# Attention plus MLP on one core: the per-unit maxima as one block-diagonal product of three float32r passes, placed between scores and products with v

## The chip, the cores and the metric

The kernel runs on one core of one Trainium2 chip. The metric is device time in microseconds (us), as the median of several runs; lower is better. Before the change it is 872.64 us (three runs, 872.33 to 872.99).

## The reference, cut to what matters

```python
xn = _layernorm(x)                        # x: 1 x 2048 x 448
q = (xn @ wq) -> 16 heads of Dh = 28;  k = xn @ wk;  v = xn @ wv     # one k and v for all heads
p = softmax(q k^T * Dh**-0.5);  o = p v                              # 2048 queries x 2048 keys per head
out = x + o @ wo + relu(xn @ w1) @ w2                                # w1: 448 x 1792
```

All of it is float32. A softmax does not change when one number is taken from all scores of a query. The kernel takes away a maximum over the first 32 keys only, so that the exponentials stay in range; any number near the true maximum would do. A flag at the end has the whole program run a second time with a maximum over all keys, if the sums have gone out of range. That second program (`HM == 64`) is built, but is not executed in the runs here.

## The kernel before, in words

**Stages.** First come the layer norm, the projections to q, k and v (each float32 number is split into a high and a low float32r part, `hi` and `lo`), and the MLP. They fill the span up to about 340 us. The attention follows, from 340 us to the end.

**Attention.** It is cut into 16 units, one for each of 4 query blocks (512 queries) and 4 groups of 4 heads. A unit has two halves of 8 key blocks (128 keys). In a half, TensorE (PE) makes 32 score tiles of 128 keys by 512 queries (L627), then the products with v (L496). The order of the scores is written out by hand in `HALVES`: `a` is a score tile that ScalarE (ACT) turns into exponentials straight from PSUM (L653, 19 in a half); `d` is a score tile that VectorE (DVE) copies from PSUM (L658, 13 in a half), and whose exponentials ACT makes later in SBUF (L673). `F` is one tile of the output projection of an earlier unit (L542, added up by DVE on L544). `R` starts the reciprocals (L517) and the normalization of the unit before.

**PSUM.** The `a` tiles have four buffers. The `d` tiles, the output projections, the maxima and the accumulator of the products with v share a ring of four banks, `d0` to `d3`: `d_tile()` takes the next name from the ring and puts it at the ring's end; the accumulator takes one with `keep=True`, and it comes back to the ring only when DVE has copied the accumulator out (`oS`, L499). So in all halves but the first unit's first, three banks go round, and a matmul into a ring tile waits until the tile three uses before it has been read.

**Operands.** `kst` holds the keys on 114 partitions: 28 rows of `hi`, 28 of `hi`, 28 of `lo`, 28 of `lo`, and two rows of ones. `qst[u]` holds a unit's queries against it: 28 rows each of `hi`, `lo`, `hi`, `lo` for four heads, loaded by four DMAs (`load_stack`, L377), and two rows for minus the maximum. A score is one float32r product over 114 rows.

**Maxima.** `maxima(u + 1)` runs in the first half of unit u, in the run of products with v, behind the first of them (`n == 1`, which is the last key block of unit u - 1). It takes one ring tile and makes, for each of the four heads, the scores of the first 32 keys in float32 (L387: 112 rows, 32 columns, 512 queries; a head has its own 32 columns of the array and 32 partitions of the tile). A float32 product is two matmul instructions in the profile. DVE then transposes (L404), reduces (L405), splits into two parts and transposes back (L406 to L408), and eight small DMAs put the result into the two rows of `qst[u + 1]` (L412). `maxima(0)` runs in the MLP.

**What sets the order.** Each engine works through its instructions in the program's order. All DMAs are issued by SyncE (SP), in that order. The pool of the attention's small tiles (`opool`, L476) lies where the MLP's tiles were; its first write, the memset of `wo` on GpSimd (POOL, L481), waits for the last matmul of the MLP.

Of the kernel before, what the change touches and what calls it, by code (L numbers as in the profile page):

```python
# [8 lines left out]
F32 = mybir.dt.float32  # L9
F32R = mybir.dt.float32r  # L10
# [36 lines left out]
def program(ctx: ExitStack, tc: tile.TileContext, HM, fine, x, wq, wk, wv, wo, w1, w2, out):  # L47
    nc = tc.nc
    P = 128
    S, D = x.shape  # L50
    DH = wk.shape[1]
# [3 lines left out]
    QB = 512  # L55
    NQB = S // QB
    TPB = QB // P
    HG = 4
# [12 lines left out]
    KQ = 4 * DH  # L71
    NU = NQB * NHG
    NA, ND, NST = 4, 4, 3
# [9 lines left out]
    def d_tile(keep=False):  # L83

        name = ring.pop(0)
        if not keep:
            ring.append(name)
        t = psD.tile([P, QB], F32, name=name)
        return (t, name) if keep else t
# [26 lines left out]
    qscr = dram.tile([NHG, 2, P, S], F32, name="qscr")  # L116
# [25 lines left out]
    MQ = HG * DH  # L142
# [53 lines left out]
    kstF = kst.bitcast(F32)  # L196
# [170 lines left out]
    units = [(b, g) for b in range(NQB) for g in range(NHG)]  # L367

    def load_stack(u):
        if u >= NU:  # L370
            return
        b, g = units[u]
        st = stacks.tile([P, HG, QB], F32R, name="qst")
        qst[u] = st
        for r in range(4):
            src = qscr[g, r % 2, 0:MQ, b * QB : (b + 1) * QB].rearrange("(j d) q -> d j q", d=DH)
            nc.sync.dma_start(st.bitcast(F32)[r * DH : (r + 1) * DH], src)  # L377

    def maxima(u):

        st = qst[u]

        def scores(kb):
            pm = d_tile()
            for j in range(HG):
                c = slice(32 * j, 32 * j + 32)
                nc.tensor.matmul(  # L387
                    pm[c], kstF[0:KQ, kb * 32 : kb * 32 + 32], st.bitcast(F32)[0:KQ, j], start=True, stop=True
                )
            return pm  # L390

        n = QB // 32
        nm = small.tile([P, n], F32, name="nm")
        nm2 = small.tile([P, 2, n], F32R, name="nm2")
        rows = small.tile([P, 2 * n], F32, name="rows")
        sc = scores(0)
        if HM > 1:
            top = small.tile([P, QB], F32R, name="tmp").bitcast(F32)
            nc.vector.tensor_copy(top, sc)
            for kb in range(1, HM):  # L400
                nc.vector.tensor_tensor(top, top, scores(kb), op=ALU.max)
            sc = top
        mt = small.tile([P, QB], F32R, name="tmp").bitcast(F32)
        nc.vector.transpose(mt, sc)  # L404
        nc.vector.tensor_reduce(nm, mt.rearrange("p (c k) -> p c k", k=32), axis=AX.X, op=ALU.max, negate=True)  # L405
        nc.vector.tensor_copy(nm2[:, 0], nm)  # L406
        nc.vector.tensor_tensor(nm2[:, 1], nm, nm2[:, 0].bitcast(F32), op=ALU.subtract)
        nc.vector.transpose(rows, nm2.rearrange("p s n -> p (s n)").bitcast(F32))  # L408
        for j in range(HG):
            for s in range(2):  # L410
                r = KQ + s
                nc.sync.dma_start(  # L412
                    st.bitcast(F32)[r : r + 1, j].rearrange("o (c q) -> o c q", q=32),
                    rows[32 * j + s * n : 32 * j + s * n + n],
                )
# [59 lines left out]
    ppool = ctx.enter_context(tc.tile_pool(name="ppool", bufs=P_BUFS, reuse_waits="tile"))  # L475
    opool = ctx.enter_context(tc.tile_pool(name="opool", bufs=2))  # L476

    g3 = opool.tile([P, NHG, D], F32, name="wo", bufs=1)
    woH = opool.tile([P, NHG, D], F32R, name="woH", bufs=1)
    woL = opool.tile([P, NHG, D], F32R, name="woL", bufs=1)  # L480
# [8 lines left out]
    def pv(u, kb, p):  # L489
        start, stop = kb == 0, kb == NKB - 1  # L490
        done = stop or u == NU - 1 and kb == KH - 2
        if start:
            o_acc[u] = d_tile(keep=True)
        o = o_acc[u][0]
        for j in range(HG):
            nc.tensor.matmul(o[32 * j : 32 * j + 32], vtile[:, kb, :], p[:, j], start=start, stop=done)  # L496
        if stop:
            oS = opool.tile([P, QB], F32, name="oS")
            nc.vector.tensor_copy(oS, o)  # L499
            ring.append(o_acc.pop(u)[1])  # L500
            o_sb[u] = oS
            dens(u)
# [32 lines left out]
    def o_proj(u, i):  # L535

        b, g = units[u]
        oH, oL = o_hl[u]
        py = d_tile()[:, 0:D]
        c = slice(i * P, (i + 1) * P)  # L540
        for n, (om, wm) in enumerate(((oH, woH), (oH, woL), (oL, woH))):
            nc.tensor.matmul(py, om[:, c], wm[:, g, :], start=n == 0, stop=n == 2)  # L542
        t = b * TPB + i
        nc.vector.tensor_tensor(acc[:, t, :], py, acc[:, t, :], op=ALU.add)  # L544
        if g == NHG - 1:
            nc.sync.dma_start(out[t * P : (t + 1) * P, :], acc[:, t, :])
# [21 lines left out]
    def last_run(u, run):  # L568

        for h, c in enumerate(halves):  # L570
            o = psA.tile([P, QB], F32, name="a")
            for n, (v, kb, p) in enumerate(run):
                for j in range(HG):
                    nc.tensor.matmul(  # L574
                        o[32 * j : 32 * j + 32, c], vtile[:, kb, :], p[:, j, c],
                        start=n == 0, stop=n == len(run) - 1,
                    )
            nc.vector.tensor_tensor(fin["o"][:, c], o[:, c], fin["o"][:, c], op=ALU.add)
            quotients(h, fin["o"][:, c])
# [39 lines left out]

    HALVES = "adadaadadaadadaFaaddadaaFadaaddaad", "adadadaadaaddaadaFadaadadaFaadaRdad"
    HA, KH = 19, NKB // 2
    todo, behind, ended = [], [], []

    def score(u, kb, j, p, pt):
        nc.tensor.matmul(  # L627
            pt, kst[0 : KQ + 2, kb * P : (kb + 1) * P], qst[u][0 : KQ + 2, j, :], start=True, stop=True
        )
        return p[:, j]  # L630

    def ends():

        for u in ended:
            recips(u)
            normalized(u)
            todo.extend((u, i) for i in range(TPB))
        ended.clear()

    for u in range(NU):  # L640
        last = u == NU - 1
        for half, order in enumerate(HALVES):
            ps, n_a, n_d = {}, 0, HA
            for k in order:
                if k in "ad":
                    n = n_a if k == "a" else n_d
                    kb, j = n // HG, n % HG
                    if kb not in ps:
                        ps[kb] = ppool.tile([P, HG, QB], F32, name="p")
                if k == "a":  # L650
                    pt = psA.tile([P, QB], F32, name="a")
                    p = score(u, half * KH + kb, j, ps[kb], pt)
                    nc.scalar.activation(p, pt, AF.Exp, scale=SCALE)  # L653
                    n_a += 1
                elif k == "d":
                    pt = d_tile()
                    p = score(u, half * KH + kb, j, ps[kb], pt)
                    nc.vector.tensor_copy(p, pt)  # L658
                    n_d += 1
                elif k == "R":  # L660
                    ends()
                else:
                    for _ in range(3 if last and half else 1):
                        if todo:
                            o_proj(*todo.pop(0))
            if last:
                ends()
            if half == 0 and u:
                load_stack(u + NST - 1)
            for c in halves if last and half else [slice(0, QB)]:  # L670
                for kb in range(HA // HG, KH):
                    p = ps[kb][:, max(HA - kb * HG, 0) : HG, c]
                    nc.scalar.activation(p, p, AF.Exp, scale=SCALE)  # L673
            run = behind + [(u, half * KH + kb, ps[kb]) for kb in range(KH)]
            behind = [] if half and u >= NU - 2 else [run.pop()]
            if last and half:
                last_run(u, run)
                break
            for n, (v, kb, p) in enumerate(run):
                if half == 0 and n == 1 and not last:  # L680
                    maxima(u + 1)
                pv(v, kb, p)
                if kb == NKB - 1:
                    ended.append(v)
            if last:
                put_by(u)
# [27 lines left out]
```

## Time and profile before

| | |
|---|---|
| median of three runs | 872.64 us (872.33 to 872.99) |
| the profiled execution | 873.85 us |
| its span, first to last instruction | 872.0 us |
| mean granted TensorE clock | 0.999 |
| maxima, L387 | 128 matmul instructions, 593 ns mean each (several overlap) |
| scores, L627 | 1024 matmul instructions (608 into `a`, 416 into `d`) |
| products with v, L496 | 1976 matmul instructions |

A row of a timeline holds the start in us from the span's beginning, the time from the first start to the last end, the engine, the line, the operation with out<-in, and a count if equal instructions follow each other; in brackets stands how long the engine was idle before it, and what ended that. PE are the matmuls, PEld the loads of their stationary operand, SPq the issues of DMAs. The duration of a matmul reaches over the start of the next ones, so that the pace is read from starts.

### The profile page before, as it was taken

Reading aid. Unit: us, or ns where it says so; the run is one execution under the profiler, and the core shown is the slowest. Engines: PE = TensorE matmul, PEld = TensorE weight load, DVE = VectorE, ACT = ScalarE, POOL = GpSimd, SP = SyncE. Lnnn points to the kernel's source line nnn. Section 1 sums busy time; section 2 is a strip of 40 time slices with the busy share of each in tenths; the row PEclk is TensorE's granted clock in tenths of the full one; section 3 lists DMA queues with packets and bytes.
Section 4 is the critical chain, followed back from the end, with each engine's and each line's share of the span. In section 5 each row is a group of like instructions: output and inputs, shape, how many; then the busy total and the mean of one; then the engine's idle time right before and its main releaser. Section 6 shows DMA issues by size and latency. Waiting matters only on the chain.

```text
span 872.0 us, 13147 instructions
## 1 busy us (share of the span) xinstructions
PE 864.4 (99%) x5062; PEld 580.1 (67%) x5062; DVE 488.9 (56%) x893; ACT 554.9 (64%) x856; POOL 112.2 (13%) x93
## 2 busy tenths in 40 slices
PE   9999999999999999999999999999999999999997
PEld 8788888888888887455455455465465465465464
DVE  6843343343333346566576576576576476476475
ACT  4541111111111114999999999999999999999894
POOL 2034212020202001201001001001001001101110
PEclk9999999999999999999999999999999999999999
DMA  7858050110000001102112023112023112021001
GB/s 216 282 205 167 17 133 1 46 28 18 1 1 1 0 2 38 44 2 55 34 26 56 14 66 76 34 25 56 14 65 77 30 29 55 15 66 34 14 14 46
DMA packets 37499, 45.87 MB, mean 53 GB/s; under 512 B 13640, under 2 KB 24072, under 8 KB 37264
## 3 DMA queue, kind: packets, MB, share of 16 engines
q1 hardware_dynamic: 37432, 44.98, 20.1%
q8 instruction: 41, 0.67, 0.3%
q14 instruction: 26, 0.21, 0.1%
HBM read 32.37 MB, written 12.18 MB: 51 GB/s over the span
## 4 chain that ended last, share of the span: by engine, by line
PE 97%; DVE 1%; ACT 1%; DMA 1%; issue 0%; SPq 0%
PE d L496 25%; PE a L627 17%; PE a L204 16%; PE a L440 12%; PE d L627 11%; PE d L542 4%; PE d L440 4%; PE a L209 4%; PE d L387 2%; PE a L288 1%; DMA acc<-in_A_x 1%; PE d L258 1%; PE a L574 1%; DVE qs L272 0%; ACT p L673 0%; ACT p L653 0%
## 5 line engine op out<-in xcount | busy, mean ns | idle before, releaser
L658 DVE COPY p<-d 128x512 f32<-128x512 f32 x416 | 258.6, 681 | 164.2 <-PE d L627 162.4
L653 ACT ACTIVATE p<-a 128x512 f32<-128x512 f32 x608 | 301.5, 696 | 41.5 <-PE a L627 41.5
L496 PE MATMUL d<-p,vtile 128*32 128x512 f32 x1976 | 221.6, 594 | 0.0
L627 PE MATMUL a<-qst,kst 114*128 114x512 f32 x608 | 217.5, 403 | 0.0
L673 ACT ACTIVATE p<-p 128x2048 f32<-128x2048 f32 (+2 forms) x132 | 198.9, 1733 | 0.0
L427 ACT ACTIVATE hH<-a 128x512 fp32r<-128x512 f32 x56 | 33.5, 598 | 236.0 <-PE a L209 236.0
L627 PEld LDWEIGHTS a<-qst,kst 114*128 114x128 f32 x608 | 114.0, 187 | 63.9 <-issue 23.5
L627 PE MATMUL d<-qst,kst 114*128 114x512 f32 x416 | 156.3, 394 | 0.0
L496 PEld LDWEIGHTS d<-p,vtile 128*32 128x32 f32 x1976 | 60.9, 110 | 140.9 <-issue 128.5
L428 DVE SCALAR_TENSOR_TENSOR hL<-a,hH 128x512 fp32r<-128x512 f32 x56 | 38.7, 691 | 118.5 <-ACT hH L427 118.5
L204 PE MATMUL a<-xH,w 128*128 128x512 f32 x408 | 104.8, 392 | 0.2 <-ACT xH L260 0.2
L440 PE MATMUL a<-w,hH 128*128 128x448 f32 x336 | 95.6, 366 | 0.0
L627 PEld LDWEIGHTS d<-qst,kst 114*128 114x128 f32 x416 | 78.3, 188 | 14.0 <-DVE p L658 3.0
L204 PEld LDWEIGHTS a<-xH,w 128*128 128x128 f32 x408 | 76.1, 188 | 16.4 <-DVE acc L447 0.8
L528 POOL TENSOR_TENSOR on<-rb,oS 128x512 f32<-128x512 f32 x15 | 19.3, 1288 | 442.6 <-DMA rb<-rscr 442.6
L447 DVE TENSOR_TENSOR acc<-a,acc 128x448 f32<-128x448 f32 x84 | 52.2, 621 | 33.8 <-PE a L440 33.8
L440 PEld LDWEIGHTS a<-w,hH 128*128 128x128 f32 x336 | 63.0, 188 | 6.4
L440 PE MATMUL a<-w,hL 128*128 128x448 f32 x168 | 61.2, 364 | 0.0
L204 PE MATMUL a<-xL,w 128*128 128x512 f32 x204 | 57.7, 390 | 0.1
L204 PEld LDWEIGHTS a<-xL,w 128*128 128x128 f32 x204 | 38.3, 188 | 8.8 <-DVE xL L261 0.7
L209 PE MATMUL a<-xR,w 128*128 128x512 f32 x136 | 42.0, 390 | 0.2 <-DVE xR L266 0.2
L544 DVE TENSOR_TENSOR acc<-d,acc 128x448 f32<-128x448 f32 x60 | 36.5, 612 | 0.0
(106 smaller groups left out, 586.0 us busy)
## 6 DMA issues: line engine op xcount, KB each, us to landing
qst<-qscr SPq DMA_DIRECT2D x64, 224.0 KB
qscr<-qs SPq DMA_DIRECT2D x16, 512.0 KB
rb<-rscr SPq DMA_DIRECT2D x60, 64.0 KB
acc<-in_A_x SPq DMA_DIRECT2D x16, 224.0 KB
out<-acc SPq DMA_DIRECT2D x16, 224.0 KB
stg<-in_B_w SPq DMA_DIRECT2D x7, 448.0 KB
stg<-in_B_w SPq DMA_DIRECT2D x7, 384.0 KB
qst<-rows SPq DMA_DIRECT2D x128, 2.0 KB
```

What stands on the lines that cost most here:

```text
L204: nc.tensor.matmul(ps, lhs[:, wi, c, cols], xm[:, c, xs], start=n == 0, stop=False)
L209: nc.tensor.matmul(ps, lhs[:, wi, DC, cols], xR[:, xs], start=False, stop=wi == 1)
L428: nc.vector.scalar_tensor_tensor(hL[:, f], ph, 0.0, hH[:, f].bitcast(F32), op0=ALU.max, op1=ALU.subtract)
L440: nc.tensor.matmul(py[:, 0:D], hm[:, f, i * P : (i + 1) * P], wd[:, wi, f, :], start=n == 0, stop=n == 3 * FC - 1)
L447: nc.vector.tensor_tensor(acc[:, t, :], py[:, 0:D], acc[:, t, :], op=ALU.add)
L496: nc.tensor.matmul(o[32 * j : 32 * j + 32], vtile[:, kb, :], p[:, j], start=start, stop=done)
L542: nc.tensor.matmul(py, om[:, c], wm[:, g, :], start=n == 0, stop=n == 2)
L544: nc.vector.tensor_tensor(acc[:, t, :], py, acc[:, t, :], op=ALU.add)
L627: nc.tensor.matmul(pt, kst[0 : KQ + 2, kb * P : (kb + 1) * P], qst[u][0 : KQ + 2, j, :], start=True, stop=True)
L653: nc.scalar.activation(p, pt, AF.Exp, scale=SCALE)
L658: nc.vector.tensor_copy(p, pt)
L673: nc.scalar.activation(p, p, AF.Exp, scale=SCALE)
```

## The change

The maxima of units 1 to 15 are made in another way, by `HM == 1` alone. A new tile `kd` (112 partitions, `hi` and `lo`, 128 columns) is set to zero once and gets the first 32 keys four times, in blocks down the diagonal: rows 28 j to 28 j + 27 (head j) against columns 32 j to 32 j + 31. A new tile `mq[u]` (two buffers) holds the queries of all four heads of a unit on 112 partitions, `hi` and `lo`; one DMA of 458,752 bytes loads it. The maxima's scores are then three accumulating float32r matmuls over the full array, `hi` by `hi`, `hi` by `lo` and `lo` by `hi`, where there were four float32 products in column groups, eight instructions.

The call of `maxima(u + 1)` moves too: from behind the first product with v to ahead of all of them, directly behind the half's last score. The copies of `kd` and the first load of `mq` stand ahead of the loads of `wo`; the later loads of `mq` (two units ahead) stand behind those of `qst`.

```diff
+    def load_mq(u):
+        if u < NU and HM == 1:
+            b, g = units[u]
+            mq[u] = opool.tile([MQ, 2, QB], F32R, name="mq")
+            src = qscr[g, :, 0:MQ, b * QB : (b + 1) * QB]
+            nc.sync.dma_start(mq[u].bitcast(F32), src.rearrange("s r q -> r s q"))
...
         def scores(kb):
             pm = d_tile()
+            if u in mq:
+                mst = mq.pop(u)
+                for n, (k, q) in enumerate(((0, 0), (0, 1), (1, 0))):
+                    nc.tensor.matmul(pm, kd[:, k], mst[:, q], start=n == 0, stop=n == 2)
+                return pm
             for j in range(HG):
...
+    if HM == 1:
+        kd = opool.tile([KQ, 2, P], F32R, name="kd", bufs=1)
+        nc.gpsimd.memset(kd.bitcast(F32), 0.0)
+        for j in range(HG):
+            for s in range(2):
+                nc.sync.dma_start(
+                    kd.bitcast(F32)[j * DH : (j + 1) * DH, s, 32 * j : 32 * j + 32],
+                    kstF[2 * s * DH : (2 * s + 1) * DH, 0:32],
+                )
+    load_mq(1)
     g3 = opool.tile([P, NHG, D], F32, name="wo", bufs=1)
...
-            if half == 0 and u:
-                load_stack(u + NST - 1)
+            if half == 0:
+                if u:
+                    load_stack(u + NST - 1)
+                load_mq(u + 2)
+                if not last:
+                    maxima(u + 1)
...
-            for n, (v, kb, p) in enumerate(run):
-                if half == 0 and n == 1 and not last:
-                    maxima(u + 1)
+            for v, kb, p in run:
                 pv(v, kb, p)
```

PE's rows at the end of unit 8's first half, before. The first three rows are the last ring tiles of the scores (`d0`, `d1`, `d3` are ring banks, the number behind is the tile's); `d2_5145` is the accumulator of unit 7, `d1_5495` that of unit 8.

```order
L627 MATMUL d0_5438<-qst_4753,kst_130 128x512
L627 MATMUL d1_5441<-qst_4753,kst_130 128x512
L627 MATMUL a_5444<-qst_4753,kst_130 128x512
L627 MATMUL a_5447<-qst_4753,kst_130 128x512
L627 MATMUL d3_5450<-qst_4753,kst_130 128x512
L496 MATMUL d2_5145<-p_5255,vtile_90 32x512 x4
L387 MATMUL d0_5476<-qst_5103,kst_130 32x512 x4
L496 MATMUL d1_5495<-p_5339,vtile_90 32x512 x4
L496 MATMUL d1_5495<-p_5363,vtile_90 32x512 x4
```

The same place with the change (the lines have new numbers: L654 are the scores, L521 the products with v, L398 the maxima).

```order
L654 MATMUL d2_5458<-qst_4771,kst_130 128x512
L654 MATMUL d3_5461<-qst_4771,kst_130 128x512
L654 MATMUL a_5464<-qst_4771,kst_130 128x512
L654 MATMUL a_5467<-qst_4771,kst_130 128x512
L654 MATMUL d1_5470<-qst_4771,kst_130 128x512
L398 MATMUL d2_5483<-mq_5127,kd_2596 128x512 x3
L521 MATMUL d0_5165<-p_5275,vtile_90 32x512 x4
L521 MATMUL d3_5516<-p_5359,vtile_90 32x512 x4
L521 MATMUL d3_5516<-p_5383,vtile_90 32x512 x4
```

The maxima's tile is in both the bank of the half's third-last ring tile (`d0_5438` before, `d2_5458` now). Before, a product with v stood between the last score and the maxima; now nothing does.

SP's rows between the MLP and unit 1, before: the results of `maxima(0)`, the loads of `wo`, the results of `maxima(1)`, the load of the stack of unit 3.

```order
L412 DMA qst<-rows 1x16x32 x8
L484 DMA wo<-in_A_wo 28x4x448 x4
L412 DMA qst<-rows 1x16x32 x8
L377 DMA qst<-qscr 28x4x512 x4
L511 DMA d<-oS 32x1x16 x4
```

The same place with the change.

```order
L427 DMA qst<-rows 1x16x32 x8
L498 DMA kd<-kst 28x32 x8
L387 DMA mq<-qscr 112x2x512
L509 DMA wo<-in_A_wo 28x4x448 x4
L387 DMA mq<-qscr 112x2x512
L427 DMA qst<-rows 1x16x32 x8
L377 DMA qst<-qscr 28x4x512 x4
```

Nine issues stand ahead of those of `wo` now, and a second load of `mq` behind them. In each later unit one load of `mq` stands behind the loads of `qst`, and the eight DMAs of the maxima's results stand ahead of the four that take the sums out of `oS` (L511 before).

More of the change, by code (lines that the diff above doesn't have):

```diff
@@ L377, in load_stack @@
             nc.sync.dma_start(st.bitcast(F32)[r * DH : (r + 1) * DH], src)
+    mq = {}
+    def load_mq(u):
[4 more added lines that the diff above has]
+            nc.sync.dma_start(mq[u].bitcast(F32), src.rearrange("s r q -> r s q"))
     def maxima(u):
```

## Prediction

> **What bounds the kernel now.** I read the page's busy shares and its chain first, then PE's timeline around one maxima, then the other engines there.
>
> ```profile
> PE 864.4 (99%) x5062; PEld 580.1 (67%) x5062; DVE 488.9 (56%) x893; ACT 554.9 (64%) x856; POOL 112.2 (13%) x93
> PE 97%; DVE 1%; ACT 1%; DMA 1%; issue 0%; SPq 0%
> PE d L496 25%; PE a L627 17%; PE a L204 16%; PE a L440 12%; PE d L627 11%; PE d L542 4%; PE d L440 4%; PE a L209 4%; PE d L387 2%; PE a L288 1%; DMA acc<-in_A_x 1%; PE d L258 1%; PE a L574 1%; DVE qs L272 0%; ACT p L673 0%; ACT p L653 0%
> ```
>
> PE carries 97% of the chain, and the maxima (L387) are 2% of the chain, in 16 pieces. PE's timeline at the end of unit 8's first half:
>
> ```profile
> 607.03 0.62 PE L627 MATMUL d<-qst,kst 114*128 114x512 f32 x2
> 607.48 0.62 PE L627 MATMUL a<-qst,kst 114*128 114x512 f32 x2
> 607.94 0.40 PE L627 MATMUL d<-qst,kst 114*128 114x512 f32 x1
> 608.27 1.06 PE L496 MATMUL d<-p,vtile 128*32 128x512 f32 x8
> 609.15 1.04 PE L387 MATMUL d<-qst,kst 112*32 112x512 f32 x8
> 610.01 6.19 PE L496 MATMUL d<-p,vtile 128*32 128x512 f32 x56
> ```
>
> There is no gap in it: four scores in 607.94 - 607.03 = 0.91 us (0.23 each), the first product with v 0.88, the maxima 610.01 - 609.15 = 0.86, then the other products. ACT at the starts of unit 8's halves, and of unit 0's second:
>
> ```profile
> 600.00 9.41 ACT L653 ACTIVATE p<-a 128x512 f32<-128x512 f32 x19 [0.59 <-PE a L627]
> 616.73 9.42 ACT L653 ACTIVATE p<-a 128x512 f32<-128x512 f32 x19 [1.44 <-PE a L627]
> 355.92 9.41 ACT L653 ACTIVATE p<-a 128x512 f32<-128x512 f32 x19 [0.43 <-PE a L627]
> ```
>
> ACT waits for PE at the start of each, so what PE gains or loses inside a half moves the end one for one, as long as a half shrinks by less than 0.43 us.
>
> **The product itself.** Three float32r passes replace the 0.86 us. A pass has the size of a score, 0.23 us; passes that accumulate in one bank, as these do, stand in the projections:
>
> ```profile
> 327.49 1.52 PE L204 MATMUL a<-xH,w 128*128 128x512 f32 x6
> 328.85 0.84 PE L204 MATMUL a<-xL,w 128*128 128x512 f32 x3
> ```
>
> Six in 1.36 us is 0.227, the same. I take 3 x 0.23 = 0.69: -0.17 us a unit, -2.55 us in 15 units. The change from the full array to column groups (0.33 us from the last score's start to the first product's, against 0.23 for a next score) is made once a half, before and after: nothing.
>
> **The wait for a ring bank.** The maxima's tile lies in the bank of the half's third-last ring tile. Before, 0.88 us of products stood between the last score and the maxima, and covered DVE's reading of that bank. Now nothing does. DVE at that place, its last four copies:
>
> ```profile
> 606.84 2.50 DVE L658 COPY p<-d 128x512 f32<-128x512 f32 x4
> ```
>
> A copy takes 0.69 us and they start (2.50 - 0.69) / 3 = 0.60 apart, so the third-last ends at 606.84 + 0.60 + 0.69 = 608.13. What PE does with a bank that comes late is to be seen in unit 5's second half, where DVE lags: DVE's copies, the weights loads that waited for the first and the third of them, and the matmuls behind those.
>
> ```profile
> 519.27 3.68 DVE L658 COPY p<-d 128x512 f32<-128x512 f32 x6 [4.96 <-PE d L627]
> 520.01 0.19 PEld L627 LDWEIGHTS d<-qst,kst 114*128 114x128 f32 x1 [0.26 <-DVE p L658]
> 521.21 0.19 PEld L627 LDWEIGHTS d<-qst,kst 114*128 114x128 f32 x1 [0.41 <-DVE p L658]
> 520.36 0.62 PE L627 MATMUL a<-qst,kst 114*128 114x512 f32 x2
> 521.55 0.63 PE L627 MATMUL a<-qst,kst 114*128 114x512 f32 x2
> ```
>
> The first copy ends at 519.96, the third at 519.27 + 2 x 0.60 + 0.69 = 521.16. The weights load follows each by 0.05 us, and the matmul behind the waiting one starts 0.34 us after that load. So the wait sits on the weights load, and the load is not hidden. In unit 8: load at 608.18, second pass at 608.52. Without a wait the second pass would start two paces behind the last score, at 607.94 + 0.46 = 608.40. The wait costs 0.12 us and leaves 0.05 of the 0.17. DVE paces this (13 copies and two additions in a row), and the copies stand to the last score in units 2 to 14 as here: 13 x 0.12 = +1.56 us. Unit 1's half has no output projection, and DVE lags less:
>
> ```profile
> 378.98 1.89 DVE L658 COPY p<-d 128x512 f32<-128x512 f32 x3 [0.21 <-PE d L627]
> 379.54 0.40 PE L627 MATMUL d<-qst,kst 114*128 114x512 f32 x1
> ```
>
> The third-last copy ends at 379.67, the load at 379.72, the second pass at 380.06 instead of 380.00: +0.06. In unit 0 four banks go round, and the bank is free early: 0.
>
> [...]
>
> **The first load of `mq` and `kd`.** It has no lead. The MLP's end, SP's and POOL's rows there, and unit 0's last score:
>
> ```profile
> 339.94 1.59 POOL L481 MEMSET wo<- 128x1792 f32 x1 [68.96 <-PE a L440]
> 347.87 1.69 POOL L485 TENSOR_SCALAR woH<-wo 128x1792 fp32r<-128x1792 f32 x1 [6.34 <-DMA wo<-in_A_wo]
> 317.25 5.00 SPq L412 DMA_DIRECT2D qst<-rows  x8
> 341.56 1.66 SPq L484 DMA_DIRECT2D wo<-in_A_wo  x4
> 348.05 0.40 PE L627 MATMUL d<-qst,kst 114*128 114x512 f32 x1
> ```
>
> And what the DMA engines moved while `wo` came (last two columns: share, GB/s):
>
> ```profile
> 341.50:342.50 1.00, 1.00 (x6) 0.75 (x6) 1.00 (x3) 1.00 (x3) 0.03 (x1) 1.00 0.00 0
> 342.50:343.50 1.00, 1.00 (x5) 0.54 (x4) 1.00 (x3) 1.00 (x3) 0.00 (x0) 1.00 0.81 203
> 343.50:344.50 1.00, 1.00 (x4) 0.61 (x4) 0.62 (x2) 1.00 (x3) 0.00 (x0) 1.00 0.96 212
> 344.50:345.50 1.00, 1.00 (x6) 0.62 (x4) 0.93 (x2) 1.00 (x4) 0.00 (x0) 1.00 0.88 208
> 345.50:346.50 1.00, 1.00 (x4) 0.48 (x3) 0.95 (x2) 1.00 (x4) 0.00 (x0) 1.00 0.87 171
> 346.50:347.50 1.00, 1.00 (x4) 0.67 (x4) 0.69 (x1) 1.00 (x4) 0.00 (x0) 1.00 0.11 18
> ```
>
> `kd`'s memset waits for the same matmul as `wo`'s did, so it starts at 339.94; by its size it takes 1.59 x 256 / 1792 = 0.23 us, to 340.2. Then SP issues eight copies of `kd` and the load. Eight copies from SBUF to SBUF (L412) were issued 0.63 us apart, loads from DRAM (L484) 0.42. `kd` is copied from SBUF to SBUF, so I take 0.63: the load is issued at 340.2 + 5.0 = 345.2. The loads of `wo` show the rest: first bytes 1.0 us after the issue (341.56 to 342.5), about 208 GB/s, and 1.2 us from the last bytes (346.6) to the waiting instruction. For 458,752 bytes: 346.2 + 2.2 + 1.2 = 349.6. The second pass then starts at 349.6 + 0.34 = 349.94 instead of 348.05 + 0.46 = 348.51: +1.43 us, once. With issues 0.42 apart, the load comes at 347.9, in time: 0. Those are the two ends.
>
> [...]
>
> **What is hidden.** SP now issues the maxima's eight DMAs ahead of the four of `oS`:
>
> ```profile
> 610.19 2.44 SPq L511 DMA_DIRECT2D d<-oS  x4
> 612.73 5.80 SPq L412 DMA_DIRECT2D qst<-rows  x8
> 624.83 0.24 DVE L517 RECIPROCAL r<-d 128x16 f32<-128x16 f32 x1
> ```
>
> They swap: the eight from about 611.5 to 617.3, the four to 619.7, and the reciprocal wants them at 624.8. About five us are left for their landing; without that slack DVE's copies would stall behind L517, and PE behind those. The later loads of `mq` have a whole unit (32.6 us) for 2.2 us of transfer. DVE makes the maxima's steps before the copy of `oS` instead of after it, in a stretch in which it idles for over 4 us.
>
> **The sum.** -2.55 + 1.56 + 0.06 + 1.43 = +0.50 us. On the profiled execution that is 873.85 + 0.50 = 874.35; that execution is 1.2 above the median of the runs, so the forecast is 872.64 + 0.50 = 873.1 us. About 0.2% (1.75 us) is what a measurement of this kernel can tell from no change; this is less.
>
> **The rivals.**
> - The first load comes in time (issues 0.42 apart, or faster bytes): the term of 1.43 goes, 871.7 us. For it speaks that all plain loads here are issued at that pace; against it, that the only rows from SBUF to SBUF are not. Chance 0.2.
> - The bank costs nothing, because the load of weights runs ahead: 1.62 goes. With the late first load 871.5, with both in time 872.64 - 2.55 = 870.1, faster than the bound. Against it stand the two waiting loads. Chance 0.1, half of it for each.
> - Slower: `mq`'s first transfer shares the DMA engines with the four of `wo` issued 0.4 to 1.7 us behind it, and ends with them. 458,752 + 802,816 bytes at 208 GB/s take 6.1 us from 346.2, with 1.2 to use: 353.5; PE stands for 5.3 us in the middle of unit 0, and the sum is -2.55 + 1.62 + 5.3 = +4.4, 877.0 us. It is slower than the bound once `mq` comes later than 350.9. For it speaks that the engines were at a share of 0.8 to 0.96 with `wo` alone; against it, that DMAs of one queue were issued in order and `mq` is ahead. Chance 0.12.
> - That the change does not do what it says is excluded by PE's rows: three instructions where eight were.
>
> **How the numbers follow.** The forecast keeps 0.58. The range, 871.4 to 874.6, holds it with both ends of the first load and a us more, and the first rival; it leaves out the slow one and half of the second, 0.17. Faster by over 0.2% has 0.07 (both waits absent, and a little for what I don't see), slower 0.15 (the shared transfer, and the forecast's upper tail), within 0.2% the rest, 0.78.
>
> **What would show it.** Right: in units 2 to 14 three matmuls from `mq` 0.23 us apart, the weights load of the first waiting for DVE by some 0.2 us behind the last score; from the last score to unit u's second product with v 0.05 us less than before; in unit 0 a wait of over 1 us for a DMA, SP's eight copies of `kd` over 5 us. Wrong: no wait on that load and units shorter by 0.17 us, a load of `mq` that lands after 351 us, or PE waiting for L517's chain.

## The result, and the profile after

The changed kernel takes 879.02 us (median of 6 runs, 876.55 to 880.13), the kernel before in the same measurement 872.78 us (6 runs, 872.33 to 873.29). The ratio is 1.0068, with a 95% interval of 1.0055 to 1.0082: slower by 6.2 us, and outside the range of the prediction. The profiled execution took 878.22 us, with a span of 876.4 (before 873.85 and 872.0), so the spans are 4.4 us apart.

The page first, the chain's shares by engine:

```profile
PE 96%; DVE 1%; SPq 1%; ACT 1%; DMA 1%; issue 0%; POOL 0%; POOLq 0%
```

Before, SPq stood last with 0% and POOL was absent; now 1% of the chain are issues of SP, and POOL is in it. The place is unit 0. PE's timeline there, from the last score of its first half (L654) over the maxima (L398) and the products with v (L521) to the first score of the next half:

```profile
347.34 0.40 PE L654 MATMUL d<-qst,kst 114*128 114x512 f32 x1
352.23 1.62 PE L398 MATMUL d<-mq,kd 112*128 112x512 f32 x3 [4.49 <-DMA wo<-in_A_wo]
353.77 7.00 PE L521 MATMUL d<-p,vtile 128*32 128x512 f32 x56
360.70 0.50 PE L654 MATMUL a<-qst,kst 114*128 114x512 f32 x1
```

The first pass starts 4.89 us after the last score. From the first of the 56 products behind it to the next half's first score are 6.93 us (353.77 to 360.70), for which the runs below need 6.1. From last score to next first score are 13.36 us. The next half's start in PE's timeline of before:

```profile
355.38 0.50 PE L627 MATMUL a<-qst,kst 114*128 114x512 f32 x1
```

Before they were 355.38 - 348.05 = 7.33 us. So unit 0 has lost 6.03 us.

The bracket names a load of `wo`, but L398 doesn't read `wo`. When several semaphores are waited for, the row names the one that came last by the profile; here the instruction needs `kd` and `mq`. What SP issued, and what POOL did at the same time:

```profile
339.23 0.31 POOL L495 MEMSET kd<- 112x256 f32 x1 [68.96 <-PE a L455]
...
355.99 1.69 POOL L510 TENSOR_SCALAR woH<-wo 128x1792 fp32r<-128x1792 f32 x1 [14.91 <-DMA wo<-in_A_wo]
339.57 6.45 SPq L498 DMA_DIRECT2D kd<-kst  x8
346.07 0.53 SPq L387 DMA_DIRECT2D mq<-qscr  x1
346.71 2.72 SPq L509 DMA_DIRECT2D wo<-in_A_wo  x4
349.48 0.38 SPq L387 DMA_DIRECT2D mq<-qscr  x1
```

Eight issues for `kd` stand 0.81 us apart (346.07 - 339.57 = 6.50 for eight), and only then is `mq` issued, at 346.07. From there to the first pass are 6.16 us. By the trace's landing events (one entry for each part of a load that has arrived) the last copy of `kd` was there at 347.2, so `mq` alone was waited for. `wo` was first read at 355.99, so PE did not wait for the end of `wo`.

Besides the two waits, for the issue and for the data, there is a third loss. It shows in the windows: busy shares by engine with counts, then the granted TensorE clock, the DMA share and GB/s.

```profile
352.00:353.00 1.00, 0.78 (x2) 0.71 (x3) 0.00 (x0) 1.00 (x2) 0.00 (x0) 0.50 1.07 177
353.00:354.00 1.00, 1.00 (x6) 0.32 (x9) 0.12 (x1) 1.00 (x1) 0.00 (x0) 0.50 1.00 158
...
355.00:356.00 1.00, 1.00 (x12) 0.24 (x8) 0.88 (x4) 0.00 (x0) 0.01 (x1) 0.80 0.34 113
```

The clock falls to half at 352.0, just as PE starts again (352.23), and is back at 355.4 (0.80 in the slice from 355 is 0.4 us of half and 0.6 of full). The three passes take 353.77 - 352.23 = 1.54 us, where they take 0.79 in the first experiment below, at a clock of 1.00.

The other units do what the prediction said. Unit 8's end of the first half, PE with the weights load of the maxima, and DVE's last four copies:

```profile
612.62 0.40 PE L654 MATMUL d<-qst,kst 114*128 114x512 f32 x1
612.87 0.96 PE L398 MATMUL d<-mq,kd 112*128 112x512 f32 x3
613.77 2.78 PE L521 MATMUL d<-p,vtile 128*32 128x512 f32 x24
612.87 0.53 PEld L398 LDWEIGHTS d<-mq,kd 112*128 112x128 f32 x3 [0.30 <-DVE p L685]
611.52 2.49 DVE L685 COPY p<-d 128x512 f32<-128x512 f32 x4
```

The third-last copy ends at 611.52 + 0.60 + 0.69 = 612.81, and the load of `kd` starts 0.06 later, idle for 0.30. From the last score to the products are 1.15 us; with the first product's 0.88 behind them that is 2.03, where before took 610.01 - 607.94 = 2.07. Weights loads that waited, over the whole span (total us, times, longest):

```profile
PEld d L398 <- issue: 4.9, 1, 4.9
PEld d L398 <- DVE p L685: 4.1, 14, 0.3
```

One wait of 4.9 us in unit 0, and one of 0.3 in each of the 14 units behind it. The chain of waits gives the length of those units, as the second half's run of products in units 1 and 14, after and before:

```profile
401.77 7.00 PE d L521 x64
...
824.93 8.06 PE d L521 x72
```

```profile
396.56 7.00 PE d L496 x64
...
820.54 8.06 PE d L496 x72
```

Thirteen units take 423.16 us after and 423.98 before: 0.06 us less for each. Now the spans add up: the MLP ended 0.71 us earlier in this execution (339.23 against 339.94 at POOL's memset, which the change does not explain: in the other runs' profiles that memset starts between 338.84 and 339.80, and at 339.18 where only the old maxima are moved), unit 0 lost 6.03, and all that follows its first half gained (876.4 - 360.70) - (872.0 - 355.38) = -0.92. The sum is +4.4.

### The profile page after: what moved, and what is told of

The parts are those of the page before. It is cut to its first block, busy times and chain, and to the rows that moved or that the text cites. A ratio compares the mean times of both kernels' runs of the same rounds, so it can differ in the third digit from the quotient of the medians.

```text
span 876.4 us, 13020 instructions
## 1 busy us (share of the span) xinstructions
PE 864.5 (99%) x4987; PEld 582.9 (67%) x4987; DVE 484.5 (55%) x893; ACT 555.1 (63%) x856; POOL 112.5 (13%) x94
## 4 chain that ended last, share of the span: by engine, by line
PE 96%; DVE 1%; SPq 1%; ACT 1%; DMA 1%; issue 0%; POOL 0%; POOLq 0%
PE d L521 25%; PE a L654 17%; PE a L204 16%; PE a L455 12%; PE d L654 11%; PE d L567 4%; PE d L455 4%; PE a L209 4%; PE d L398 2%; PE a L288 1%; PE d L114 1%; SPq L498 1%; PE d L258 1%; DMA wo<-in_A_wo 1%; PE a L599 1%
## 5 line engine op out<-in xcount | busy, mean ns | idle before, releaser
L521 PE MATMUL d<-p,vtile 128*32 128x512 f32 x1976 | 219.6, 595 | 0.0
L654 PE MATMUL a<-qst,kst 114*128 114x512 f32 x608 | 217.3, 403 | 0.0
L654 PEld LDWEIGHTS a<-qst,kst 114*128 114x128 f32 x608 | 113.9, 187 | 64.7 <-issue 24.3
L654 PE MATMUL d<-qst,kst 114*128 114x512 f32 x416 | 155.8, 393 | 0.0
L521 PEld LDWEIGHTS d<-p,vtile 128*32 128x32 f32 x1976 | 60.8, 110 | 142.1 <-issue 130.7
L654 PEld LDWEIGHTS d<-qst,kst 114*128 114x128 f32 x416 | 78.2, 188 | 13.4 <-DVE p L685 2.3
```

Source lines behind the costliest of these rows:

```text
L654: nc.tensor.matmul(pt, kst[0 : KQ + 2, kb * P : (kb + 1) * P], qst[u][0 : KQ + 2, j, :], start=True, stop=True)
```

## The experiments

The theory after the result: the whole loss lies in unit 0, in the wait for the first `kd` and `mq` and in the clock that the wait costs. The rivals: that sharing the DMA engines with `wo` makes the wait, that the clock's fall costs nothing of its own, and that the steady units lose too, by the new place of the maxima or by the ring bank.

**The first load early.** `kd` and `mq` get a pool of their own (`early`) that doesn't wait for the MLP's end, and are loaded within the MLP. The rest is the changed kernel.

```diff
+    early = ctx.enter_context(tc.tile_pool(name="early", bufs=2, side="right"))
...
         if n == 8:
             for u in range(NST):
                 load_stack(u)
+            if HM == 1:
+                kd = early.tile([KQ, 2, P], F32R, name="kd", bufs=1)
+                nc.gpsimd.memset(kd.bitcast(F32), 0.0)
...
+            load_mq(1)
```

> kd and all loads of mq lie in a pool of their own, and kd and the first mq are filled in the MLP. Theory A (the whole loss is unit 0's wait for the first kd and mq, and the fall of PE's clock behind it): PE waits for nothing in unit 0, the clock stays at 1.00, units stay 0.04 to 0.05 us shorter than before, and the time is 0.5 to 1.2 us under before, about 871.9, 7 us under the changed kernel's 879.0. Theory B (the maxima's new place and the traffic of mq cost in every unit): the time stays within 2 us of the changed kernel's 879.0.

871.89 us (11 runs, 871.24 to 872.26); against the kernel before 0.9987, interval 0.9978 to 0.9996. PE in unit 0:

```profile
346.94 0.39 PE L656 MATMUL d<-qst,kst 114*128 114x512 f32 x1
347.18 0.86 PE L400 MATMUL d<-mq,kd 112*128 112x512 f32 x3
347.97 6.21 PE L523 MATMUL d<-p,vtile 128*32 128x512 f32 x56
354.11 0.50 PE L656 MATMUL a<-qst,kst 114*128 114x512 f32 x1
```

The maxima follow the last score by 0.24 us, and the stretch takes 7.17 us, 6.19 less than in the changed kernel and 0.16 less than before. The profiled executions differ by 6.6 us (878.22 and 871.62), the medians by 7.1. The loss is in unit 0.

**PE kept busy through the wait.** The changed kernel with 16 throw-away score products ahead of unit 1's maxima, into the maxima's bank (the first pass has `start` set). They change no wait for DMA, only what PE does during it.

```diff
                 mst = mq.pop(u)
+                for _ in range(16 if u == 1 else 0):
+                    nc.tensor.matmul(pm, kst[0 : KQ + 2, 0:P], qst[0][0 : KQ + 2, 0, :], start=True, stop=True)
```

> The changed kernel, with 16 score matmuls (3.7 us) whose results are thrown away, ahead of unit 1's maxima, where PE waits for mq. Theory A1 (the fall of the clock to one half for 3.4 us behind the wait costs 1.7 us of its own): the maxima start where they did, PE's clock stays at 1.00 in unit 0, and the time is 1.7 us under the changed kernel, about 877.3. Theory A2 (the wait alone costs, the slow clock is hidden or only recorded): the time stays at 879.0, or rises where the load comes before the 16 matmuls are through.

877.04 us (5 runs, 875.83 to 877.23); ratio 1.0044, interval 1.0031 to 1.0058. PE's timeline in unit 0:

```profile
347.31 3.81 PE L398 MATMUL d<-qst,kst 114*128 114x512 f32 x16
352.06 0.93 PE L400 MATMUL d<-mq,kd 112*128 112x512 f32 x3 [0.94 <-issue]
352.92 6.22 PE L523 MATMUL d<-p,vtile 128*32 128x512 f32 x56
359.07 0.50 PE L656 MATMUL a<-qst,kst 114*128 114x512 f32 x1
```

And a window of it, to be held against the one from 353 of the changed kernel:

```profile
353.00:354.00 1.00, 1.00 (x12) 0.34 (x16) 0.94 (x2) 1.00 (x1) 0.00 (x0) 1.00 0.96 200
```

The data come as late as in the changed kernel (352.06 here, 352.23 there), but the clock stays at 1.00, the three passes take 0.86 us instead of 1.54, and maxima and products take 359.07 - 352.06 = 7.01 us instead of 8.47. So the clock costs about 1.5 us by the rows and 2.0 by the medians, whose ranges overlap (876.55 to 880.13 and 875.83 to 877.23), and the wait the rest.

**Only `kd` early.** `kd` is filled within the MLP, as in the first experiment; `mq`'s first load stays behind the MLP, ahead of `wo`.

```diff
+            if HM == 1:
+                kd = early.tile([KQ, 2, P], F32R, name="kd", bufs=1)
...
-    if HM == 1:
-        kd = opool.tile([KQ, 2, P], F32R, name="kd", bufs=1)
...
     load_mq(1)
```

> Only kd is filled in the MLP; the first load of mq stays behind the MLP, ahead of the loads of wo. Theory A3 (SP's eight issues of kd, 0.8 us apart, are what makes mq late): mq is issued at about 339.3 instead of 346, lands by 345, and there is no wait: 871.9. Theory A4 (the shared transfer with wo is what makes it late): mq lands only with the last of wo, at 347 to 349, and PE waits 0 to 1.5 us: 872 to 873.5.

872.30 us (11 runs, 871.48 to 873.33); ratio 0.9992, interval 0.9983 to 1.0001. SP's rows there, then PE's:

```profile
339.00 0.34 SPq L389 DMA_DIRECT2D mq<-qscr  x1
340.65 1.65 SPq L511 DMA_DIRECT2D wo<-in_A_wo  x4
```

```profile
347.14 0.39 PE L656 MATMUL d<-qst,kst 114*128 114x512 f32 x1
347.37 0.87 PE L400 MATMUL d<-mq,kd 112*128 112x512 f32 x3
```

`mq` is issued 7 us earlier, `wo` follows 1.65 us behind it, and PE does not wait for a DMA there. Without the eight issues of `kd` the load has 8.4 us from its issue to its use, and this is enough. So these issues are what the loss hangs on.

**`wo` out of the way.** The changed kernel with `wo`'s memset, loads and split (L506 to L511) moved to the start of unit 1, so that nothing of it moves beside the first `mq`.

```diff
-    nc.gpsimd.memset(g3, 0.0)
+    def load_wo():
+        nc.gpsimd.memset(g3, 0.0)
...
+        if u == 1:
+            load_wo()
```

> The loads of wo (and what GpSimd makes of them) move to the start of unit 1; kd and mq stay where the change put them. If the transfers of wo slow that of mq (A4): mq lands 3.7 us behind its issue, at 349.8 instead of 351.9, PE waits some 2.3 us instead of 4.5, its clock stays at 1.00 if the wait is short enough, and the time falls by 2 to 4 us, to 875 to 877. If they don't (A3 alone): 879.0, unchanged.

877.85 us (5 runs, 876.64 to 879.5); ratio 1.0061, interval 1.0047 to 1.0075. SP's issues and PE's timeline in unit 0:

```profile
339.45 6.46 SPq L498 DMA_DIRECT2D kd<-kst  x8
345.95 1.04 SPq L387 DMA_DIRECT2D mq<-qscr  x2
```

```profile
351.31 1.04 PE L398 MATMUL d<-mq,kd 112*128 112x512 f32 x3 [3.69 <-DMA mq<-qscr]
```

From issue to first pass 5.36 us instead of 6.16: sharing with `wo` costs 0.8 us by these rows, 1.2 by the medians (with the ranges overlapping). With `wo` gone the bracket names `mq`.

This run does not show the first `mq` alone, though: the second, as large, is now issued directly behind it, where `wo` stood. The trace holds 16 landing events for such a load, and they tell more. In the third experiment, with no copies ahead of `mq` and `wo` 1.65 us behind it, all 16 have come 3.90 us after the issue (342.90). Here 15 have come after 4.34 us (350.29) and the last after 5.01 (350.96). In the changed kernel 15 have come after 4.17 us (350.24) and the last after 5.80 (351.87), 0.36 us before the first pass. So beside other loads, whether `wo` or the second `mq`, the last part came 0.7 to 1.6 us behind the other 15, and PE waited for it. Why it is late is not shown.

The clock falls here too, after a shorter idle time:

```profile
351.00:352.00 1.00, 0.69 (x3) 0.48 (x3) 0.00 (x0) 1.00 (x2) 0.00 (x0) 0.99 0.02 8
352.00:353.00 1.00, 1.00 (x6) 0.20 (x8) 0.61 (x1) 1.00 (x2) 0.00 (x0) 0.50 0.00 0
```

PE starts again at 351.31 at full speed, and falls to half at 352.0 while it is at work.

The next four runs take the steady units apart. For each I give the median and, in the table behind them, what the rows of one unit say.

**The ring bank.** The early version with the maxima's tile from the four `a` buffers instead of the ring.

```diff
-            pm = d_tile()
+            pm = psA.tile([P, QB], F32, name="a") if u in mq else d_tile()
```

> As e1_early, and the maxima's tile comes from the four score banks that ACT empties (a) instead of the ring that DVE empties (d). Theory A (the first weights load waits for DVE's third-last copy, 0.12 us in units 2 to 14 and 0.06 in unit 1): ACT's fourth-last tile is read 0.3 us earlier, the wait goes, and the time falls by 1.6 us against e1_early, to about 870.3, 2.5 under before. Theory B (the second pass is late for another reason, the change from scores to maxima itself): no change against e1_early, 871.9.

869.87 us (6 runs, 869.58 to 870.63); ratio 0.9967, interval 0.9955 to 0.9979. PE in unit 8:

```profile
572.80 0.39 PE L656 MATMUL d<-qst,kst 114*128 114x512 f32 x1
573.03 0.86 PE L400 MATMUL a<-mq,kd 112*128 112x512 f32 x3
573.83 7.07 PE L523 MATMUL d<-p,vtile 128*32 128x512 f32 x64
```

Passes at 0.23 us and then the change to the products; in unit 8 no wait of the load is left, and over the whole span five loads wait for ACT, 0.8 us in all, where 14 waited for DVE, 4.1 us. Last score to products: 1.03 us instead of 1.15, the 0.12 of the prediction. The medians are 2.0 us apart (the prediction had 1.62 for the bank in all). This version is faster than both kernels.

**The place alone.** The kernel before, with its float32 maxima moved to where the change has them.

```diff
+                if not last:
+                    maxima(u + 1)
...
-            for n, (v, kb, p) in enumerate(run):
-                if half == 0 and n == 1 and not last:
-                    maxima(u + 1)
+            for v, kb, p in run:
```

> The kernel before with its float32 maxima in column groups, moved alone to the place ahead of the products with v. Theory A (the place costs only by the wait for the ring bank): the first weights load in column groups starts 0.33 us behind the last score anyway, when the bank has been free for 0.07 us, so nothing changes: 872.8, within 0.3. Theory B (the place itself costs, because DVE's copy of the accumulator and its four DMAs come behind the maxima's): over 0.5 us slower than before.

872.45 us (11 runs, 871.92 to 872.98); ratio 0.9996, interval 0.9987 to 1.0005. In unit 8:

```profile
574.15 0.39 PE L627 MATMUL d<-qst,kst 114*128 114x512 f32 x1
574.47 1.06 PE L387 MATMUL d<-qst,kst 112*32 112x512 f32 x8
575.36 1.90 PE L496 MATMUL d<-p,vtile 128*32 128x512 f32 x16
```

No difference that can be measured: SP's and DVE's new order costs nothing.

**The product at the old place.** The early version with the call behind the first product with v again.

```diff
-                if not last:
-                    maxima(u + 1)
...
+            for n, (v, kb, p) in enumerate(run):
+                if half == 0 and n == 1 and not last:
+                    maxima(u + 1)
```

> As e1_early, with the call of the maxima back behind the first product with v. Theory A (each change between the full array and column groups costs about 0.10 us, and the move saves two of them): the half gains 0.17, pays 0.21, and has no wait for a bank: 0.04 us longer than before in each of 15 units, 873.4, 1.5 over e1_early. Theory B (a change between the two costs nothing here): 872.8 - 2.55 = 870.3.

875.70 us (7 runs, 874.92 to 875.88); ratio 1.0029, interval 1.0018 to 1.0040. In unit 8:

```profile
575.90 0.40 PE L656 MATMUL d<-qst,kst 114*128 114x512 f32 x1
576.23 1.06 PE L523 MATMUL d<-p,vtile 128*32 128x512 f32 x8
577.22 0.96 PE L400 MATMUL d<-mq,kd 112*128 112x512 f32 x3
578.12 2.35 PE L523 MATMUL d<-p,vtile 128*32 128x512 f32 x20
574.82 2.48 DVE L687 COPY p<-d 128x512 f32<-128x512 f32 x4
577.22 0.53 PEld L400 LDWEIGHTS d<-mq,kd 112*128 112x128 f32 x3 [0.84 <-DVE p L687]
```

Now the array goes from column groups to the full array and back inside the run of products. A product takes 0.99 us to the maxima where 0.88 is its own time, and the maxima 0.90 to the next product where their passes are 0.69. At this place the new product is slower than the old one. The bracket of the maxima's load names DVE, but DVE's third-last copy, the one of that bank, had ended at 574.82 + 0.60 + 0.69 = 576.11, 1.1 us before the load. So the bank does not explain the 0.99. The load starts with the first pass (both at 577.22) instead of ahead of it, as a score's load does (612.39 for the last score at 612.62, in unit 8 of the changed kernel). That fits the change of the array; no run takes this apart further.

**One pass of three.** The `a`-tile version with the `hi` by `hi` pass only: the maxima are those of rounded scores.

```diff
-                for n, (k, q) in enumerate(((0, 0), (0, 1), (1, 0))):
-                    nc.tensor.matmul(pm, kd[:, k], mst[:, q], start=n == 0, stop=n == 2)
+                for n, (k, q) in enumerate(((0, 0),)):
+                    nc.tensor.matmul(pm, kd[:, k], mst[:, q], start=True, stop=True)
```

> As e5_a_tile, with the first of the three passes alone (hi by hi). The maxima are then those of rounded scores; the softmax does not change by what is subtracted, so the kernel still computes the reference. Theory A (every pass lies on PE's path at 0.23 us): 2 x 0.23 x 15 = 6.9 us less than e5_a_tile, 863.4 if that comes out at 870.3. Theory B (another engine is next: ACT waits for PE only 0.43 to 0.6 us at the starts of halves): less than 6.9, since a half can shrink only by that before ACT sets the pace; the whole step from before would be 0.63 us a unit, so 1 to 2 us of it could be missing.

863.14 us (4 runs, 862.68 to 863.28); ratio 0.9886, interval 0.9871 to 0.9901. In unit 8:

```profile
569.90 0.39 PE L656 MATMUL d<-qst,kst 114*128 114x512 f32 x1
570.13 0.39 PE L400 MATMUL a<-mq,kd 112*128 112x512 f32 x1
570.45 1.92 PE L523 MATMUL d<-p,vtile 128*32 128x512 f32 x16
```

6.73 us less than with three passes; 15 x 2 x 0.23 = 6.9 are the two passes. PE pays every pass in full.

Unit 8's time from the last score to the second product with v (0.88 us added where no product stands between), the difference from before times 15 units, and the difference of the medians:

| kernel | last score to second product, us | x 15 against before | medians |
|---|---|---|---|
| before | 2.07 | | |
| first load early (573.36 to 574.51) | 1.15 + 0.88 = 2.03 | -0.6 | -1.0 |
| and an `a` tile | 1.03 + 0.88 = 1.91 | -2.4 | -3.0 |
| and one pass | 0.55 + 0.88 = 1.43 | -9.6 | -9.7 |
| the place alone | 1.21 + 0.88 = 2.09 | +0.3 | -0.4 |
| first load early, old place | 2.22 | +2.3 | +2.8 |

One place in one unit accounts for each median within 0.7 us.

## Why the prediction was wrong

It forecast +0.5 us, no change that can be measured, and the kernel is 6.2 us slower. By its steps:

- **The product, -0.17 us a unit: right.** Passes at 0.23 us; two of them are worth 6.73 us in 15 units (6.9 by the rows).
- **The ring bank, +0.12 us a unit: right.** The load of `kd` waits for DVE in 14 units, and 0.12 us go when the tile lies elsewhere. Units 1 to 14 were to gain 14 x 0.17 - 1.62 = 0.76 us; the profile shows 0.92 for all that follows unit 0's first half. The rival in which the bank costs nothing is refuted: the wait is there, and taking it away gives 2.0 us.
- **What is hidden: right.** With the maxima moved alone the time is the same, and the early version, with a load of `mq` in every unit, is no slower than before.
- **The first load of `mq` and `kd`, +1.43 us: the step that failed.** With its product (-0.17), unit 0 was to lose 1.26 us, and it lost 6.03. The prediction had named a load of `mq` that lands after 351 us as a sign of being wrong, and its last part landed at 351.87. The 4.8 us are three errors. First, SP: the issue was to come 5.3 us after the MLP's end, at 0.63 us for each copy, and came 346.07 - 339.23 = 6.84 after it, at 0.81 for each, +1.6 us. Second, the way of the data: issue to first pass was to be 349.6 + 0.34 - 0.23 - 345.2 = 4.5 us and was 6.16, +1.6 us. The size fits a load with nothing close behind it (in the third experiment 3.9 us to the landing, and here 0.36 from there to the first pass); beside `wo` the last of 16 parts of `mq` landed 1.63 us after the others, and why it did stays open. Third, the clock: the prediction had no price at all for what a wait does to PE behind it, +1.5 us.

The slow rival gave 877.0 us, the nearest of the numbers, but its mechanism is only part of what happened, and the number came near by luck. `mq` shared the engines with `wo` and came 0.8 us later than with the second `mq` in `wo`'s place, yet it did not end with `wo` (352 against 356), and without `wo` the kernel is still 877.85. What the rival had right is that `mq` would come later than 350.9; what it left out are the slower issues and the clock. The first rival, `mq` in time, is what the third experiment looks like once `kd` is out of the way: 872.3, with 871.7 forecast.

The prediction had bounded the issue of `kd` by 0.42 and 0.63 us, both rows of other shapes, and took the upper row as the end of its range. Since this term had no cover at all on PE, each 0.1 us an issue was 0.8 us of the kernel, and the range had to reach beyond the rows. And a wait of PE as long as these, 3.7 and 4.5 us, has to be priced twice, once as the wait and once as the clock.

The runs of the changed kernel spread over 3.6 us, with a granted clock of 0.995 to 0.997 over the span; with PE kept busy they spread over 1.4, at 0.999 to 1.00. A second stretch of 3.4 us at half clock would cost 3.4 x 0.5 = 1.7 us, 0.002 of the span, so the clock may make this spread and the 0.5 us between rows and medians. That is an estimate: beside the stretch from 352.0, the profiled execution of the changed kernel shows half clock only behind PE's last matmul (0.50 in the slice from 875.0 to the end), where that of the kernel before has it too (0.50 from 871.0).

## What to carry to other kernels

For a constant that is built once by many small DMAs, ask where the queue has time for its issues: here eight copies of 3.5 KB, 6.50 us of issues ahead of the one load that PE needed, cost more than 15 better products brought back (6.03 us in unit 0 against 0.92 behind it), and with the copies within the MLP the loss was gone (872.30 us, ratio 0.9992). When a change adds operands, work out for the first use, not the steady state, when its last issue can leave the queue, and load it a stage earlier if the memory allows. Of a saving of 0.17 us a unit, 0.12 were eaten here by the bank that the shortened work no longer covers; taking the tile from the `a` buffers gave them back (1.03 us from last score to products instead of 1.15).

## What the runs showed of the hardware

- After an idle time of PE of 4.5 us the granted clock was 0.50 for 3.4 us (352.0 to 355.4), and after one of 3.7 us as well; there it fell 0.7 us after PE had started again. With PE kept at work and 0.9 us idle it stayed at 1.00. What sets the moment of the fall and its length is not shown.
- SP's issues of 28 x 32 copies from SBUF to SBUF stood 0.81 us apart (6.50 for eight), where those of a row stood 0.63 apart (the eight from 317.25 in the kernel before) and the issue of `mq`'s 448 KB took 0.34 to 0.53. What makes the difference was not tried.
- From full-array passes to column groups a step took 0.33 us instead of 0.23 (in the kernel before), and with the maxima inside the products unit 8 took 2.22 us from the last score to the second product where it took 2.03 at their edge; so here the product of the other shape was better put where a change is made anyway.
- A load of 448 KB landed whole 3.90 us after its issue with 1.65 us of lead over the next; with other loads directly behind it the last of its 16 parts came 0.7 us (the second `mq` behind it) and 1.6 us (`wo` behind it) after the other 15, and PE waited for that one.
